# Where a step's work stands in the output stage of a long-convolution and mixture-of-experts kernel: number lists fetched later, measuring at the step's head, exponentials first

## The chip, the cores and the metric

The kernel runs on one core of a Trainium2 chip. The metric is device microseconds (us) of one launch, the median of several runs. Engines are named as the profile names them: PE (TensorE matmuls), PEld (its weight loads), DVE (VectorE), ACT (ScalarE), POOL (GpSimd) and SP (SyncE, which here only issues DMAs). Each engine works through its own instructions in order; between engines there are semaphores.

## The reference, cut to what matters

```python
def _attn_ref(x, v, pos_emb, w1, w2):            # x, v: 4 x 11456 x 128
    h_filt = (np.maximum(pos_emb @ w1, 0.0) @ w2) * np.exp(-0.01 * pos)[:, None]
    u = x * v
    ...                                           # y = causal convolution of u with h_filt, by FFT
    return x * y

def _moe_ref(x, w_skip, w_gate, w1, w2):          # x: 45824 x 128, 8 experts of 128 x 1024 x 128
    do_compute = x @ w_skip > 0                   # the others pass unchanged
    logits = xc @ w_gate
    e_idx = np.argmax(logits, axis=1)             # one expert for each token
    ...                                           # gate_w: its softmax probability
    for e in range(E):
        y[mask] = gate_w[mask, None] * (np.maximum(xc[mask] @ w1[e], 0.0) @ w2[e])
    out[do_compute] = xc + y
```

Everything is float32. The convolution's result is the input of the expert layer; which token goes to which expert is known only once its row of the convolution is there.

## The kernel before, in words

The program has four stages, one after the other. `first_phase` and `freq_phase` do the forward transforms and the product with the filter's spectrum; the change doesn't touch them. `out_phase` does the last transform, writes the rows, sorts the tokens to experts and begins the experts' work. `late_slots` does the rest of the experts.

`out_phase` goes through 32 chunks of 1,536 rows. A chunk's work is a set of small functions, each put at a *step* (the chunk's first step plus a lag) and at a rank within the step; the table of `(lag, order, f)` at lines 1336 to 1340 sets both. Chunks begin at steps 0, 4, 7 and then every third step (`START`, `first`), so chunk 2 begins at step 7, chunk 6 at 19, chunk 7 at 22 and chunk 8 at 25. Within a step the functions are issued in order of rank, and this is the order of the instructions on every engine. At rank 0.5 of every step (`PACE`: and now and then once more at the step's end) the generator `work` is advanced by one `yield`: that is the experts' work of `early_slots`, one part of a unit at a time.

What a chunk goes through: `produced` (lag 0: L1111 on PE multiplies with the transform, L1112 on DVE multiplies with x into the tile `xm`; the next loads of `ox` and half of the next `zt` are issued on SP), `turned` (lag 1, L1124: 12 transposes), `score` (lag 3, L1133, then ACT's copy `lt`, L1135), `score2` (lag 4, L1140), `choose` (lag 5, DVE: best expert, L1151 makes `df`), `exp` (L1165, ACT), `gate` (L1170 to L1172, DVE: writes the gate value into `xm`), `count` and `total` (PE: how many tokens go to each expert), `full` (L1191, DVE), `measure` (L1198, PE) and `measured`, `ranks` and `route`, `spread` (L1242, DVE), `collect` (L1250, PE), `write` (L1256, L1257 on DVE, then L615: POOL writes the chunk's token numbers to the lists in DRAM, one list for each expert). `store` writes `xm` to the output (SP, L1116). PE's products, scores and transposes share three PSUM buffers (`wide`, L1062), and the small results (`mine`, `whole`, `sizes`, `rk`, `tabs`) share one bank (L1034 to L1038).

The experts work in *slots* of 256 tokens of one expert. Which expert a slot takes, and where its numbers lie in the lists, is a *table*, made after chunks 2, 4, 8, 13, 22, 28 and 31 (`KNOWN`, `ex.table`, L557 to L606) in five *links* that alternate between DVE and PE; `tabled` advances it, up to two links a step. `name` then issues on SP the DMA that fetches a slot's 256 numbers (`ids<-lists`, L625), at most two slots a step, and not before the step after the chunk's list was written. `ex.more` issues on POOL the indirect DMAs that gather the rows by these numbers (`xt<-out,ids`, L667), one slot a step. `prepare` waits until a unit's slots are named, and for the first unit two more steps; then PE transposes the gathered rows (L719) and the unit's matmuls follow (L730 to L732 up, L813 down). 18 units of the first 28 slots belong to `early_slots`; what `out_phase` doesn't reach is done at its end without a chunk beside it (L1345 to L1356), and the other 61 slots and four half ones come in `late_slots`.

Of the kernel before, what the change touches and what calls it, by code (L numbers as in the profile page):

```python
# [44 lines left out]
NKNOWN = sum(n * u for c, n, u in KNOWN)  # L45
# [5 lines left out]
QX = 4  # L51
PACE = 1.24
START = (0, 4, 7)
STORE = 7
C4 = 2
XM = 4
ZT = 3
ZB = 2
# [4 lines left out]
NHALF = 4  # L63
NLAST = NEARLY + NLATE - NKNOWN
NTAB = 188
HALF = NKNOWN + NTAB
IDLE = 512
FRONT = 7
# [420 lines left out]
class Experts:  # L489
# [255 lines left out]
    def early_slots(self, pool, work, psum, bank):  # L745

        nc = self.nc

        def up(w, hl, u):
            n = hl.shape[2]  # L750
            hp = bank512()
            nf = 2 * T // n
            for f in range(nf):
                self.up(w, hl, hp[:, f * n:(f + 1) * n], u * nf + f)
            h = work.tile([128, 2 * T], F32, name="h", bufs=8)
            nc.scalar.activation(h, hp, AF.Relu)
            return [h[:, f * n:(f + 1) * n] for f in range(nf)]

        def bank512():
            return psum.tile([128, 2 * T], F32, name="mh")  # L760

        got, w, hl, wd = {}, {}, {}, {}
        self.ahead = got, w, hl

        self.now, seen = 0, []

        def gather(s, most=XT):
            while most and len(seen) < s + GATHERS and len(seen) in self.names:
                n = len(seen)
                seen.append(n)  # L770
                got[n] = self.gather(n, self.ids[:, n], pool, self.names[n])
                most -= 1

        self.more = lambda: gather(self.now, 1)

        def prepare(u):

            s = self.now = u[0]
            while not all(n in self.names for n in u):
                yield  # L780
            gather(s, max(u[-1] + 1 - len(seen), 0))
            if s not in hl:
                for _ in range(4 if s else 2):
                    yield
                w[s] = self.split(got[s][0], pool, 0, nc.vector)
                hl[s] = self.turn([got[n] for n in u], pool, bank512())
                yield
                if s:
                    yield
        for u, then in zip(BEFORE, BEFORE[1:] + UNITS[:1]):  # L790
            yield from prepare(u)
            s, k = u[0], then[0]
            sts = [got.pop(n) for n in u]
            wd[s] = work.tile([128, F], F32, name="wd", bufs=1)
            nc.scalar.copy(wd[s], self.w2f[:, ds(self.where(nc.scalar, sts[0][0]), F)])
            h, parts = [], 4 * len(u)
            for part in range(parts):
                h += up(w[s], hl[s], part)
                if part % 2 and part < parts - 1:
                    yield  # L800
            del w[s], hl[s]
            ready = all(n in got for n in then)
            if ready:
                w[k] = self.split_high(got[k][0], pool, 0)
                hp = bank512()
                hl[k] = self.turn_high([got[n] for n in then], pool, hp)
            yield
            if ready:
                self.turn_low(hl[k], hp)
                self.split_low(w[k], got[k][0], 0, nc.vector)  # L810
            for j in range(2 * len(u)):
                for f in range(F // 128):
                    nc.tensor.matmul(bank[:, j * D:(j + 1) * D], h[f][:, j * 128:(j + 1) * 128],  # L813
                                     wd[s][:, f * D:(f + 1) * D], start=(f == 0), stop=(f == F // 128 - 1))
                if j < 2 * len(u) - 1:
                    yield
            del wd[s]
            for m, (tb, xt, ids, since) in enumerate(sts):
                o = self.row()
                for j in range(2):  # L820
                    self.gated(o[:, j, 0:D], bank[:, (2 * m + j) * D:(2 * m + j + 1) * D], xt, j)
                    self.store(o[:, j], ids, j, since)
            yield
        yield from prepare(UNITS[0])

    def late_slots(self, pool):
# [205 lines left out]
def out_phase(tc, i, out, zd, ex, consts):  # L1032
# [6 lines left out]
    with (  # L1039
        tc.tile_pool(name="slot", bufs=2, reuse_waits="tile") as eb,  # L1040
    ):
      with (
# [16 lines left out]
        tabs = bank[0][:, 136:136 + 2 * NTAB]  # L1059
        revb = rev[:, None, :].broadcast_to([128, NT, E])  # L1060

        chunks = {}  # L1062
# [18 lines left out]
        def load_z(ch, p, heads=NP):  # L1081

            if ch < NCH:
                if ch not in zts:
                    zts[ch] = oz.tile([128, 2 * NP, NS * DH], F32, name="zt", bufs=ZB)
                rows = slice(p * NP, p * NP + heads)
                nc.sync.dma_start(zts[ch][:, rows], zs[2 * K1 * ch:2 * K1 * ch + 128, rows])
# [79 lines left out]
        def gate(ch):  # L1167
            xm, oh, ee, df = chunks[ch]
            sm = ob.tile([128, NT], F32, name="sm")
            nc.vector.tensor_reduce(sm, ee, axis=AX.X, op=ALU.add)  # L1170
            nc.vector.scalar_tensor_tensor(sm, sm, 1e-9, sm, ALU.add, ALU.max)
            nc.vector.reciprocal(xm[:, :, D], sm)  # L1172
            chunks[ch] = oh

        def count(ch):

            oh = chunks[ch][1]
            nc.tensor.matmul(mine, oh.rearrange("p e t -> p (e t)"), ones[:, 0:1], start=True, stop=True)

        def counted(ch):  # L1180
# [42 lines left out]
        def route(ch):  # L1223

            oh = chunks.pop(ch)
            sel = ob.tile([128, E, NT], F32, name="sel", bufs=1)
            nc.vector.scalar_tensor_tensor(sel, rk.rearrange("p (e t) -> p e t", t=NT), (PL + 1) / 2 / PL, oh, ALU.subtract, ALU.mult)
            rs = ob.tile([128, NT], F32, name="rs")
            nc.vector.tensor_reduce(rs, sel.rearrange("p e t -> p t e"), axis=AX.X, op=ALU.add)
            tf = ob.tile([128, 2, NT], F16, name="tf")  # L1230
            nc.vector.scalar_tensor_tensor(tf[:, 0], rs, WHOLE, wholes, ALU.add, ALU.subtract)
            nc.vector.tensor_tensor(tf[:, 1], rs, tf[:, 0], ALU.subtract)
            chunks[ch] = tf
# [27 lines left out]
        cr, cts, written, checks, base, at = {}, {}, {}, {}, 0, [0]  # L1261
# [16 lines left out]
        tables = []  # L1278
# [6 lines left out]
        def name(most=2):  # L1285

            for s, ch in fresh:
                ex.names[s] = ch
            fresh.clear()
            for _ in range(most):  # L1290
                if not groups:
                    return
                s, ch, b = groups[0]
                if b not in ex.tabled or written.get(ch, at[0]) >= at[0]:
                    return
                groups.pop(0)
                ex.issue(s, ch)
                fresh.append((s, ch))

        started = []  # L1300

        def tabled(half):

            if tables and (not half or started):
                started.append(1)
                if next(tables[0], tables) is tables:
                    tables.pop(0)
                    started.clear()

        def routed(ch):  # L1310
            route(ch)
            last = ch == NCH - 1
            if not last and ch in checks:
                tables.append(ex.table("full", *checks[ch], ob, tabs))
            if last:
                tables.append(zip_longest(ex.table("most", *checks[ch], ob, tabs), ex.table("half", HALF, NHALF, 1, ob, tabs[:, 64:])))
                tables.append(ex.table("last", NKNOWN, NTAB, 1, ob, tabs))

        def produced(ch):
            for blk in range(NB):  # L1320
# [11 lines left out]
        steps = {}  # L1332
        for ch in range(NCH):
            for blk in range(NB):
                steps.setdefault(first(ch) + blk + STORE, []).append((9, store, (ch, blk)))
            for lag, order, f in (
                    (0, 0, produced), (1, 0.1, lambda ch: load_z(ch + ZB, 1)), (1, 4, turned),
                    (3, -0.1, score), (4, 2, score2), (5, 3, choose), (6, 1, exp), (6, 4.5, count), (6, 6, counted), (6, 6, gate), (7, 4.4, total),
                    (8, -2.5, full), (8, 4.4, measure), (8, 4.5, ranks),
                    (9, -2.3, measured), (9, -2, routed), (11, -2.4, spread), (12, 0.2, collect), (12, 0.3, lay), (12, 2.5, laid), (12, 2.6, write)):  # L1340
                steps.setdefault(first(ch) + lag, []).append((order, f, (ch,)))
        for t in steps:
            steps[t] += [(-1.5, tabled, (0,)), (4.7, tabled, (1,)), (7.5, name, ()), (7.6, lambda: ex.more(), ())]
        credit = 0.0
        for t in sorted(steps):  # L1345
            at[0] = t
# [105 lines left out]
```

## Time and profile before

| | |
|---|---|
| median of 3 runs | 1577.55 us (1574.77 to 1578.71) |
| the profiled execution | 1581.42 us, of which its span is 1579.6 us |
| PE busy | 1484.2 us, 94% of the span |
| DVE, POOL, ACT busy | 72%, 68%, 48% |
| mean granted clock of TensorE | 0.973 of full speed |

The span is from the first instruction to the last; 1.8 us lie around it. Shares are means over stages with different limits, so the section with rows shows stretches of the span by themselves. A wait is told as "waiting engine and line <- what ended the wait". The granted clock is 1.00 at 2.4 GHz and 0.50 at 1.2 GHz.

### The profile page before, as it was taken

What the parts mean: (1) busy time and instruction counts of PE and PEld (TensorE: products, weight loads), DVE (VectorE), ACT (ScalarE), POOL (GpSimd) and SP (SyncE); (2) the same over time, 40 slices, a digit from 0 to 9 for tenths busy, and PEclk for the clock granted to TensorE, in tenths of its full rate; (3) what the DMA queues carried; (4) which work ended last, traced back from release to release, by engine and by line L of the source; (5) the groups of instructions that cost most, each with busy time, mean ns of one, the idle gap of its engine ahead of it and who ended that gap; (6) DMA issues with size and microseconds to landing.
All of it is one profiled execution on the core that took longest, in us unless ns stands there. A gap on an engine that the chain in (4) does not pass through costs nothing. (4 is left out here: it accounts for less than half of the span.)

```text
span 1579.6 us, 24184 instructions
## 1 busy us (share of the span) xinstructions
PE 1484.2 (94%) x7360; PEld 931.2 (59%) x7360; DVE 1130.7 (72%) x2323; ACT 755.1 (48%) x1509; POOL 1080.7 (68%) x832
## 2 busy tenths in 40 slices
PE   8976999999999999998759999999989999999998
PEld 3542444444444444443437767777777888888888
DVE  2324877888788889996757877777766777777774
ACT  5542555544545444442224554444535555555554
POOL 2102988888888878882157566875777888888756
PEclk9996999999999999999789999999989999999999
DMA  9998999999999978978968888988521111111100
GB/s 322 332 337 316 382 372 375 359 331 331 314 353 330 311 237 271 351 202 286 352 193 259 252 276 263 283 282 249 174 63 35 46 46 45 46 46 43 43 25 29
DMA packets 200376, 361.82 MB, mean 229 GB/s; under 512 B 64492, under 2 KB 140762, under 8 KB 200206
## 3 DMA queue, kind: packets, MB, share of 16 engines
q1 hardware_dynamic: 181078, 317.04, 59.5%
q0 software_dynamic: 16448, 38.88, 8.5%
q10 hardware_dynamic: 2720, 4.34, 0.9%
q8 instruction: 59, 0.97, 0.3%
q14 instruction: 71, 0.58, 0.1%
HBM read 216.77 MB, written 145.42 MB: 229 GB/s over the span
## 5 line engine op out<-in xcount | busy, mean ns | idle before, releaser
L412 PE MATMUL ps<-y,c 128*128 128x512 f32 x720 | 331.3, 597 | 0.3
L480 POOL TENSOR_TENSOR y<-y,p 128x2048 f32<-128x2048 f32 x59 | 267.8, 4538 | 70.0 <-DVE p L401 70.0
L736 POOL DMA_INDIRECT out<-o,ids x182 | 199.3, 1095 | 116.3 <-DVE o L743 78.6
L412 PEld LDWEIGHTS ps<-y,c 128*128 128x128 f32 x720 | 133.4, 190 | 173.0 <-issue 156.5
L667 POOL DMA_INDIRECT xt<-out,ids x182 | 192.8, 1059 | 58.4 <-issue 29.1
L401 DVE TENSOR_TENSOR p<-xp,g 128x1024 f32<-128x1024 f32 x240 | 217.4, 948 | 0.0
L401 DVE TENSOR_TENSOR y<-xp,g 128x1536 f32<-128x1536 f32 x120 | 210.9, 1757 | 4.0
L852 DVE SCALAR_TENSOR_TENSOR hh<-hp,hh 128x1024 fp32r<-128x1024 f32 x122 | 148.7, 1219 | 88.9 <-ACT hh L851 75.5
L413 ACT COPY z<-ps 128x512 f32<-128x512 f32 x180 | 105.6, 586 | 178.3 <-PE ps L412 158.6
L851 ACT ACTIVATE hh<-hp 128x1024 fp32r<-128x1024 f32 x122 | 126.4, 1036 | 92.1 <-issue 70.4
L481 POOL TENSOR_TENSOR y<-y,p 128x1024 f32<-128x1024 f32 x59 | 139.1, 2357 | 4.6
L640 POOL MEMSET idle<- 128x512 f16 x231 | 126.3, 547 | 0.3
L381 PE MATMUL xp<-x,wf 128*128 128x480 f32 x256 | 117.4, 583 | 9.1 <-DMA x<-x1f 5.9
L210 PE MATMUL ps<-wf,c 60*120 60x384 f32 x512 | 112.6, 536 | 11.6 <-DVE wf L193 11.6
L212 ACT COPY wf<-ps 120x384 f32<-120x384 f32 x256 | 105.6, 493 | 27.0 <-PE ps L210 23.8
L813 PE MATMUL bank<-wd,h 128*128 128x128 f32 x896 | 114.8, 286 | 0.0
L193 POOL TENSOR_TENSOR wf<-wf 124x768 f32<-124x768 f32 x45 | 82.0, 1822 | 47.5 <-DVE g L394 47.4
L813 PEld LDWEIGHTS bank<-wd,h 128*128 128x128 f32 x896 | 108.0, 198 | 0.3
L730 PE MATMUL hp<-hl,ws 128*128 128x512 f32 (+1 forms) x256 | 103.2, 403 | 2.6 <-issue 1.5
L393 DVE TENSOR_TENSOR g<-xp,g 128x128 f32<-128x128 f32 x120 | 34.8, 290 | 97.2 <-ACT g L386 97.1
L384 ACT COPY g<-xp 64x192 f32<-64x192 f32 x120 | 38.0, 317 | 137.4 <-PE xp L381 94.7
L707 DVE TENSOR_TENSOR ws<-wf,ws 128x1024 fp32r<-128x1024 f32 x82 | 99.9, 1218 | 5.0 <-issue 3.2
(199 smaller groups left out, 2851.3 us busy)
## 6 DMA issues: line engine op xcount, KB each, us to landing
wf<-xv SPq DMA_DIRECT2D x64, 768.0 KB
x1d<-wf SPq DMA_DIRECT2D x64, 720.0 KB
x<-x1d SPq DMA_DIRECT2D x60, 768.0 KB
zt<-zd SPq DMA_DIRECT2D x60, 768.0 KB
zd<-z SPq DMA_DIRECT2D x110, 384.0 KB
out<-xm SPq DMA_DIRECT2D x96, 258.0 KB
ox<-xo SPq DMA_DIRECT2D x96, 256.0 KB
x1f<-fx POOLq DMA_DIRECT2D x16, 720.0 KB
```

The source lines that it names most:

```text
L210: nc.tensor.matmul(ps[p], self.c1[rows], u[rows, q * RUN:(q + 1) * RUN], start=True, stop=True)
L381: nc.tensor.matmul(xp[:, k, 0:(NS + NB) * DH], c2(n % PER * KS + j * KH + k), x1[:, j * KH + k], start=True, stop=True)
L401: nc.vector.tensor_tensor(o[:, :, :, j * KH:(j + 1) * KH].rearrange("p s a k b d -> p (s a) k b d"), x[:, None].broadcast_to([128, m, KH, ...
L412: nc.tensor.matmul(zps, c3[:, a, :], y[:, blk, a], start=(a == 0), stop=(a == 1))
L480: nc.gpsimd.tensor_tensor(y[:, 1:], y[:, 1:], p1, ALU.add)
L481: nc.gpsimd.tensor_tensor(y[:, 2:], y[:, 2:], p2, ALU.add)
L640: self.nc.gpsimd.memset(self.idle, 0.0)
L667: ins = nc.gpsimd.indirect_dma_start(out=xt[:, j], out_offset=None, in_=self.rows[0:have], in_offset=bass.IndirectOffsetOnAxis(ap=ids[:, j ...
L736: ins = nc.gpsimd.indirect_dma_start(out=self.rows, out_offset=bass.IndirectOffsetOnAxis(ap=ids[:, j:j + 1], axis=0), in_=o, in_offset=Non ...
L813: nc.tensor.matmul(bank[:, j * D:(j + 1) * D], h[f][:, j * 128:(j + 1) * 128], wd[s][:, f * D:(f + 1) * D], start=(f == 0), stop=(f == F / ...
L851: nc.scalar.activation(h[:, 0], hp, AF.Relu)
L852: nc.vector.scalar_tensor_tensor(h[:, 1], hp, 0.0, h[:, 0].bitcast(F32), ALU.max, ALU.subtract)
```

## The change

Eight edits, all in `out_phase` and `early_slots`:

- `STORE` 7 becomes 6: a block of `xm` is stored one step earlier.
- The first unit waits three steps instead of two after its numbers are named (L783).
- `name` fetches numbers two steps behind the list's writing instead of one.
- `exp` moves to the head of its step, ahead of the score's copy; `gate` from the step's end to its middle. `count` now takes the chunk's state over from `exp`.
- `measure` and `ranks` move from the end of the step at lag 8 to the head of lag 9, just ahead of `measured`.
- Tables of chunks 7 to 30 (`FRONT` is 7) advance one link a step, the others two as before; the first of the two places in a step moves from rank -1.5 to -0.1.
- `score2` moves behind the step's transposes (`turned`).
- The second half of a `zt` load moves from the next step's head to its own step's end, ahead of the stores there.

```diff
-STORE = 7
+STORE = 6
...
-                for _ in range(4 if s else 2):
+                for _ in range(4 if s else 3):
...
-            chunks[ch] = oh
...
-            oh = chunks[ch][1]
+            oh = chunks[ch] = chunks[ch][1]
...
-                if b not in ex.tabled or written.get(ch, at[0]) >= at[0]:
+                if b not in ex.tabled or written.get(ch, at[0]) >= at[0] - 1:
...
-            if tables and (not half or started):
+            if tables and (not half or started and tables[0][1]):
                 started.append(1)
-                if next(tables[0], tables) is tables:
+                if next(tables[0][0], tables) is tables:
...
-                tables.append(ex.table("full", *checks[ch], ob, tabs))
+                tables.append((ex.table("full", *checks[ch], ob, tabs), ch < FRONT))
...
-                    (0, 0, produced), (1, 0.1, lambda ch: load_z(ch + ZB, 1)), (1, 4, turned),
-                    (3, -0.1, score), (4, 2, score2), (5, 3, choose), (6, 1, exp), (6, 4.5, count), (6, 6, counted), (6, 6, gate), (7, 4.4, total),
-                    (8, -2.5, full), (8, 4.4, measure), (8, 4.5, ranks),
-                    (9, -2.3, measured), (9, -2, routed), (11, -2.4, spread), (12, 0.2, collect), (12, 0.3, lay), (12, 2.5, laid), (12, 2.6, write)):
+                    (0, 0, produced), (0, 8.9, lambda ch: load_z(ch + ZB, 1)), (1, 4, turned),
+                    (3, -0.05, score), (4, 4.2, score2), (5, 3, choose), (6, -0.5, exp), (6, 2.7, gate), (6, 4.5, count), (6, 6, counted), (7, 4.4, total),
+                    (8, -2.5, full), (9, -0.4, measure), (9, -0.35, ranks),
+                    (9, -0.3, measured), (9, -0.2, routed), (11, -2.4, spread), (12, 0.2, collect), (12, 0.3, lay), (12, 2.5, laid), (12, 2.6, write)):
...
-            steps[t] += [(-1.5, tabled, (0,)), (4.7, tabled, (1,)), (7.5, name, ()), (7.6, lambda: ex.more(), ())]
+            steps[t] += [(-0.1, tabled, (0,)), (4.7, tabled, (1,)), (7.5, name, ()), (7.6, lambda: ex.more(), ())]
```

What moves on the engines, at three places. First PE, where the first slot's gathered rows (`xt`) are transposed. Before, this is at the head of chunk 7's second step, behind a count of tokens (L1178) and one link of a table (L571, L572); `score2` and the chunk's transposes come after:

```order
L1213 MATMUL bank_4480<-ge_4482 53x1
L1178 LDWEIGHTS oh
L1178 MATMUL bank_4478<-ones,oh 96x1
L571 LDWEIGHTS shift
L571 MATMUL bank_4478<-tnt,shift 8x1
L572 LDWEIGHTS shift
L572 MATMUL bank_4478<-done,shift 8x1
L719 MATMUL mh<-ident,xt_4442 128x128 x2
L1140 MATMUL bank_4480<-ident,lt 128x128 x3
L1124 MATMUL wide<-ident,xm 128x128 x12
```

Of the change, the same transposes (L719), now at the head of chunk 8's second step, and with `score2` (L1140) behind the chunk's transposes:

```order
L1212 MATMUL bank_4480<-ge_4481 53x1
L1177 LDWEIGHTS oh
L1177 MATMUL bank_4478<-ones,oh 96x1
L719 MATMUL mh<-ident,xt_4442 128x128 x2
L1124 MATMUL wide<-ident,xm 128x128 x12
L1140 MATMUL bank_4480<-ident,lt 128x128 x3
L1185 LDWEIGHTS odd
L1185 MATMUL bank_4478<-ct,odd 96x1
L730 MATMUL mh<-hl,ws_5522 128x256
```

The first unit has moved by one chunk on PE: chunk 8's score, product and collecting now stand ahead of it.

Second SP, ahead of the first fetch of numbers (L623 loads the slot's address, L625 fetches). Before, it follows the loads that chunk 6's steps issue, with one store between the two halves of `zt`:

```order
L1078 DMA ox<-xo 128x512 x3
L1087 DMA zt<-zd 128x4x384
L1116 DMA out<-xm 128x516
L1087 DMA zt<-zd 128x4x384
L623 TENSOR_LOAD addr
L623 ISA x2
L625 REGISTER_ALU
L625 DMA ids<-lists 128x2
```

Of the change, the same place: both halves of `zt` go out together, and two stores stand between them and the first fetch:

```order
L1078 DMA ox<-xo 128x512 x3
L1087 DMA zt<-zd 128x4x384 x2
L1116 DMA out<-xm 128x516 x2
L623 TENSOR_LOAD addr
L623 ISA x2
L625 REGISTER_ALU
L625 DMA ids<-lists 128x2
```

The fetch has moved behind the stores, to just ahead of the loads that chunk 7's steps issue.

Third ACT, a chunk with a unit beside it. Before, the score's copy (`lt`) stands ahead of the unit's work (`h`, `ws`, `hl`), and `exp` (`ee`) behind it:

```order
L1135 COPY lt<-wide 128x384
L756 ACTIVATE h<-mh 128x512 x2
L691 TENSOR_LOAD tb
L691 ISA x2
L702 ISA
L702 COPY ws_5577<-wf 128x1024
L721 CAST hl<-mh 128x256
L1165 ACTIVATE ee<-df 128x96
L1182 CAST ct<-bank_4478 96x1
L1142 COPY lg<-bank_4480 128x108
L1127 COPY xT<-wide 128x512 x3
```

Of the change:

```order
L702 COPY ws_5631<-wf 128x1024
L721 CAST hl<-mh 128x256
L1165 ACTIVATE ee<-df 128x96
L1135 COPY lt<-wide 128x384
L1181 CAST ct<-bank_4478 96x1
L1127 COPY xT<-wide 128x512 x3
L1142 COPY lg<-bank_4480 128x108
```

`exp` now stands directly ahead of the score's copy, and `lg` behind the three copies `xT`.

## Rows read from the trace of the kernel before

**Rows 1.** Stretches of the span: its bounds and length in us, busy us of each engine (and instructions), granted clock, busy share of the DMA engines, GB/s.

```profile
730.00:800.00 70.00, 52.93 (x352) 27.05 (x353) 46.06 (x170) 18.15 (x45) 9.82 (x10) 0.88 0.94 318
800.00:820.00 20.00, 5.37 (x34) 4.86 (x34) 6.70 (x27) 4.14 (x8) 12.59 (x14) 0.66 0.70 220
820.00:1130.00 310.00, 298.43 (x2452) 221.01 (x2451) 233.48 (x882) 145.42 (x297) 211.02 (x245) 1.00 0.82 258
1130.00:1200.00 70.00, 61.91 (x431) 50.99 (x431) 44.72 (x183) 29.61 (x49) 55.14 (x65) 0.93 0.27 64
1200.00:1500.00 300.00, 299.07 (x1412) 246.79 (x1411) 222.28 (x323) 174.03 (x204) 239.09 (x248) 1.00 0.16 44
```

**Rows 2.** Waits of PE from 700 to 1200 us: total us, times, longest us.

```profile
PE mh L719 <- DMA xt<-out,ids: 13.8, 2, 9.7
...
PE bank L1140 <- DVE pl L1257: 5.1, 4, 3.0
PE bank L1198 <- DVE tdn L599: 4.5, 3, 1.8
PE bank L1198 <- DVE tab L594: 3.9, 3, 2.1
```

**Rows 3.** Timeline of PE around the first slot's transposes: start, us, instruction, and in brackets the idle time before it and what ended it.

```profile
793.31 1.47 PE L1124 MATMUL wide<-ident,xm 128*128 128x128 f32 x12
...
800.81 0.16 PE L572 MATMUL bank<-done,shift 8*8 8x1 f16 x1
810.63 0.48 PE L719 MATMUL mh<-ident,xt 128*128 128x128 f32 x1 [9.65 <-DMA xt<-out,ids]
815.29 0.47 PE L719 MATMUL mh<-ident,xt 128*128 128x128 f32 x1 [4.19 <-DMA xt<-out,ids]
815.56 0.85 PE L1140 MATMUL bank<-ident,lt 128*128 128x128 f32 x3
816.20 2.52 PE L1124 MATMUL wide<-ident,xm 128*128 128x128 f32 x12
```

**Rows 4.** Two short stretches within that wait, columns as in rows 1.

```profile
805.00:810.00 5.00, 0.00 (x0) 0.00 (x0) 1.23 (x1) 0.00 (x0) 4.34 (x5) 0.50 0.59 147
810.00:815.00 5.00, 0.48 (x1) 0.18 (x1) 0.00 (x0) 0.00 (x0) 4.67 (x6) 0.50 1.00 329
```

**Rows 5.** Timeline of POOL there: the writing of chunk 2's list and the first two gathers.

```profile
793.18 1.59 POOL L615 DMA_INDIRECT lists<-pl,lies  x1 [7.37 <-DVE sm L1170]
...
805.28 2.12 POOL L667 DMA_INDIRECT xt<-out,ids  x1 [7.72 <-DMA ids<-lists]
...
808.12 1.02 POOL L667 DMA_INDIRECT xt<-out,ids  x1 [0.17 <-issue]
```

**Rows 6.** Timeline of SP's DMA issues there: the last load before the first fetch, and the fetch.

```profile
793.93 0.42 SPq L1087 DMA_DIRECT2D zt<-zd  x1
802.56 1.46 SPq L625 DMA_DIRECT2D ids<-lists  x2
```

**Rows 7.** Timeline of DVE: the products (L1112) of chunks 5, 6 and 7, and the wait of `full` between the first two.

```profile
777.12 1.89 DVE L1112 TENSOR_TENSOR xm<-wide,ox 128x512 f32<-128x512 f32 x3 [0.96 <-DMA out<-xm]
...
783.10 0.15 DVE L1191 TENSOR_SCALAR nt<-bank 96x1 int32<-96x1 f32 x1 [1.23 <-PE bank L587]
...
789.62 0.69 DVE L1112 TENSOR_TENSOR xm<-wide,ox 128x512 f32<-128x512 f32 x1
...
800.79 1.89 DVE L1112 TENSOR_TENSOR xm<-wide,ox 128x512 f32<-128x512 f32 x3
```

**Rows 8.** Timeline of PE in the same stretch: `score2`, `measure` and the products of chunks 6 and 7.

```profile
779.43 0.90 PE L1140 MATMUL bank<-ident,lt 128*128 128x128 f32 x3 [3.04 <-DVE pl L1257]
...
785.19 0.22 PE L1198 MATMUL bank<-ct,sums 96*128 96x2 f16 x3 [2.13 <-DVE tab L594]
...
786.96 4.79 PE L1111 MATMUL wide<-zt,c 128*64 128x512 f32 x12
...
792.92 0.55 PE L1140 MATMUL bank<-ident,lt 128*128 128x128 f32 x3 [0.63 <-DVE pl L1257]
...
796.47 2.80 PE L1111 MATMUL wide<-zt,c 128*64 128x512 f32 x12
```

**Rows 9.** Timeline of PE: the first and the last of `measure`'s waits for a table from 820 us on (of five).

```profile
821.02 0.21 PE L1198 MATMUL bank<-ct,sums 96*128 96x2 f16 x3 [0.50 <-DVE tab L594]
...
1136.72 0.21 PE L1198 MATMUL bank<-ct,sums 96*128 96x2 f16 x3 [1.78 <-DVE tdn L599]
```

**Rows 10.** Timeline of PE: score and product of one chunk with experts' work beside it.

```profile
928.76 0.85 PE L1133 MATMUL wide<-xT,wg 128*32 128x384 f32 x8
929.55 2.79 PE L1111 MATMUL wide<-zt,c 128*64 128x512 f32 x12
```

**Rows 11.** Timeline of ACT beside it: the score's copy and `exp`.

```profile
929.68 0.48 ACT L1135 COPY lt<-wide 128x384 f32<-128x384 f32 x1 [1.11 <-PE wide L1133]
931.66 0.28 ACT L1165 ACTIVATE ee<-df 128x96 f32<-128x96 f32 x1 [1.50 <-DVE df L1151]
```

**Rows 12.** Timeline of PE at the stage's end: down matmuls (L813) of the last unit but one, and the first up and the down matmuls of the last unit.

```profile
1167.44 8.41 PE L813 MATMUL bank<-wd,h 128*128 128x128 f32 x48
...
1178.44 0.50 PE L730 MATMUL mh<-hl,ws 128*128 128x512 f32 x1
...
1185.79 7.31 PE L813 MATMUL bank<-wd,h 128*128 128x128 f32 x64
```

More of the change, by code (lines that the diff above doesn't have):

```diff
@@ L1313, in routed @@
             if not last and ch in checks:
-                tables.append(ex.table("full", *checks[ch], ob, tabs))
+                tables.append((ex.table("full", *checks[ch], ob, tabs), ch < FRONT))
             if last:
-                tables.append(zip_longest(ex.table("most", *checks[ch], ob, tabs), ex.table("half", HALF, NHALF, 1, ob, tabs[:, 64:])))
-                tables.append(ex.table("last", NKNOWN, NTAB, 1, ob, tabs))
+                tables.append((zip_longest(ex.table("most", *checks[ch], ob, tabs), ex.table("half", HALF, NHALF, 1, ob, tabs[:, 64:])), True))
+                tables.append((ex.table("last", NKNOWN, NTAB, 1, ob, tabs), True))
         def produced(ch):
```

## The prediction

> **What bounds the kernel now.** I read the stretches first, then PE's waits, then the timelines around the longest of them. The reader is to see in the stretches [rows 1] three regimes of the stage that changes. From 730 to 800 us PE is busy 52.9 of 70 us, the DMA engines 0.94 and DVE 46.1: loads and DVE set the pace, not PE. From 820 to 1130 PE is busy 298.4 of 310 us and after 1200 it is 299.1 of 300: there PE is the bound, and whatever time PE loses earlier comes out at the end. Between them PE does 5.4 us of work in 20. So I price the change by the time in which PE stands still or runs slowly from 730 us on, and ask of each such wait whether it goes.
>
> The longest is the first slot's gathered rows: 13.8 us in two waits [rows 2, 3]. Behind it the granted clock is 0.50, the lower level [rows 4], and the first transposes take 2.52 us where they took 1.47 before: 1.05 us more [rows 3]. Then come `score2` waiting for DVE's `pl` (5.1 us) and `measure` waiting for the tables (4.5 and 3.9 us) [rows 2].
>
> **The change part by part.** The durations come from the profiled execution of 1581.42 us, 3.87 us above the median of the runs; I subtract from it and take the 3.87 off at the end.
>
> *Fetching later, one more step for the first unit.* Counted through the loops, chunk 2's list is written in step 19; before, the numbers are fetched at the end of step 20, gathered at the end of step 21 and used on PE in step 23; now this is 21, 22 and 26. The chain itself is long: POOL issues the list at 793.18 [rows 5]; SP, idle since 794.35, issues the fetch at 802.56 [rows 6], 9.4 us later; the first gather starts at 805.28, the second at 808.12 [rows 5], and its rows are there at 815.29 [rows 3]. That is 22.1 us from list to transposes. How much of it do the later places cover? The list is issued 3.56 us after chunk 6's first product on DVE (789.62), and PE comes to its place in step 26 at about chunk 8's product, two chunks on. Chunk 6 to 7 took 11.17 us on DVE [rows 7] and 9.51 us on PE [rows 8]. Two chunks less 3.56 are 18.8 us at the one pace and 15.5 at the other, so 3.3 to 6.6 us of the wait stay; I take 5.0, and for the range 0 to the whole 13.84. So 8.8 us go. The slow restart stays in the sum, as a wait of 3.04 us at 779 also left products at 4.79 us instead of 2.80 [rows 8]. The Trainium skill ("TensorE: Matmul & The Clock Gate", section "HAM oscillation — how this bites in real kernels") says that idle gaps throttle the array again and that each restart is paid; the trace agrees with the 4.79 us, and if the leftover wait spared it the sum would be 1.05 us lower. Against the gain stands that the units begin two steps later, in the regime where PE idles: 17.1 of 70 us [rows 1], 0.24, of two thirds of a 9.5 us chunk are 1.5 us. **First unit: 8.8 - 1.5 = 7.3 us.**
>
> What the later fetch does to SP: it now stands ahead of chunk 8's `ox`, but it is reached later, so the 8.2 us between 794.35 and 802.56, in which nothing behind it is loaded, become a wait of perhaps half as much. The Trainium skill ("DMA: Bandwidth & Descriptors", "Latency and other measured facts") puts a DMA's fixed cost at about 2 us and lower on a lightly loaded HBM. By it the list would have landed near 796.8, an estimate; the trace shows the fetch 7.8 us after POOL had issued the list, so I keep the row. By the page the leftover wait would be 0 and the sum 5.0 us lower.
>
> *Store a step earlier, `score2` behind the transposes, in the DVE-paced stretch.* Here a stall of PE is worth only what it costs DVE. DVE waited 0.96 us for an output store to free `xm` and 1.23 us for PE's total, which stood behind the waiting `score2` and the slowed transposes [rows 7, 8]. With `STORE` 6 the store has a step more, and `pl` is ready by the time the transposes are done. The rest of the 3.04 and 2.13 us is DVE's own pace and stays. **2.2 us.** Bounds: 0, and the 5.2 us of both PE waits.
>
> *One link a step, measuring at the head, `score2` later, in the PE-bound stretch.* `score2`'s waits there are 5.1 less 3.04 and 0.63 [rows 2, 8], 1.4 us; `measure`'s are 4.5 plus 3.9 less 2.13 [rows 2, 8], 6.3 us in five waits [rows 9]. A table's last link no longer stands right ahead of `measure`: it falls in a chunk's second step, and a unit's part and 12 transposes come before PE next writes that bank. All 7.7 us go. What is late next: `exp` is now ahead of the score's copy on ACT. PE's third product needs the PSUM buffer that this copy frees (three buffers, score and two products before it). In the chunk at 929 `exp` could only start at 931.66, for DVE's `df` [rows 11]; with 0.28 and 0.48 behind it the buffer is free at 932.4, and PE would want it at 929.55 + two thirds of 2.79 = 931.4 [rows 10]: a new wait of 1.0 us. DVE lags so far in few chunks; I take two such waits, 2.0 us. **5.7 us.** Bounds: 0 and 7.7.
>
> *`gate` in the middle, `count`, `measured`, the second `zt` half.* Nothing: DVE's order around `measured` is the same and PE's `measure` still precedes score and product; the `zt` half is needed two chunks later. What hides them is the experts' matmuls, and from 730 to 800 us, where there are none, they are within the 2.2 us above.
>
> *The stage's end.* The last units start three steps later and more of their matmuls fall behind the last chunk. PE does them at the same cost wherever they stand, unless it idles. From 1130 to 1200 PE idles 8.1 us at a mean clock of 0.93 [rows 1]. I take 0, bounds a gain of 5 us (70 us times 0.07 of clock) and a loss of 14 us (a rival, below).
>
> **Sum:** 7.3 + 2.2 + 5.7 = 15.2 us. 1581.4 - 15.2 = 1566.2, less 3.9 for the median: **1562 us**, 1.0% faster.
>
> **The rivals.**
>
> *The wait moves along whole.* The list may land later under a busier DMA queue: the DMA engines are at 0.94 in this stretch [rows 1] and were at 0.59 for part of the chain [rows 4]. For it: everything up to the gather is fed by a DMA. Against it: the program gives 15 to 19 us where the chain took 22. Then 8.8 us don't come: 1571 us.
>
> *The gain is used up at the end.* The last unit's matmuls took from 1178.44 to 1193.1, some 14 us, at full clock; the 48 down matmuls ahead of them took 8.41 us where 64 take 7.31 [rows 12], 0.175 us each instead of 0.114. Should PE idle so long before the last unit that it runs at half the clock throughout, its 14 us double: 1576 us. For it: three parts fewer lie beside a chunk. Against it: more experts' work, not less, then stands beside the last tables.
>
> *Slower: `exp` holds up every product.* If in each of the 24 chunks from chunk 8 on DVE is as late as at 929, PE waits 1.0 us in each for its third product: 24 us instead of the 2 counted, 1562 + 22 = 1584 us. It decides from a `df` that ends more than 1.9 us after the score's start: then 0.28 and 0.48 put the copy's end past the 2.65 us [rows 10, 11] at which the third product is due. For it: DVE is 75% busy there [rows 1]. Against it: `exp` was behind a unit's copies before, and `gate` behind that; with `exp` early DVE waits less and lags less.
>
> **How the numbers follow.** The forecast 0.66, with a range of its own from 1554 to 1570; the wait moved along 0.14, the end 0.08, slower 0.07; better than the range's lower end 0.05. A measurement of this kernel can tell 0.3%, 4.7 us, from no change. The forecast, the better case and half of the moved wait, whose 1571 lies near the bound of 1572.8, are faster: 0.78. The other half and the end are the same: 0.15. Slower: 0.07. The range goes down by the whole leftover wait and the clock at the end, 1562 - 5 - 5 = 1552, and up by the whole wait and the third term, 1562 + 8.8 + 5.7 = 1577.
>
> **What would show it.** Right: PE's wait at L719 is some 5 us instead of 13.8; `measure` and `score2` are gone from PE's list of waits; PE from 820 to 1130 is busy over 0.97; the first long matmuls of the late stage start 12 to 18 us earlier. Wrong: a wait of 10 us or more at L719; PE waiting at L1111 for ACT's `lt`; a granted clock near 0.5 for over 15 us between 1130 and 1200; SP held so long by the fetch that products wait for `ox`.

## The result, and the profile after

The changed kernel is slower: 1591.3 us, median of 7 runs (1590.81 to 1595.93), against 1577.55 us for the kernel before on the same chip (7 runs, 1572.4 to 1584.92). The ratio is 1.0096, 95% interval [1.0073, 1.0119]: 0.96% slower, where 1.0% faster was forecast and the range ended at 1577. The profiled execution took 1594.65 us, its span 1592.8 us, the mean granted clock fell from 0.973 to 0.965.

The same five stretches as in [rows 1], of the kernel after:

```profile
730.00:800.00 70.00, 55.71 (x369) 27.47 (x370) 49.22 (x185) 19.03 (x50) 10.31 (x11) 0.88 0.97 330
800.00:820.00 20.00, 13.76 (x99) 9.14 (x101) 15.93 (x57) 7.68 (x16) 18.40 (x22) 0.83 0.99 311
820.00:1130.00 310.00, 289.92 (x2305) 210.08 (x2299) 219.24 (x832) 137.41 (x284) 207.90 (x238) 0.97 0.81 249
1130.00:1200.00 70.00, 61.00 (x449) 50.77 (x450) 41.64 (x178) 25.51 (x45) 46.93 (x56) 0.90 0.25 58
1200.00:1500.00 300.00, 297.98 (x1417) 245.93 (x1416) 220.83 (x323) 171.98 (x200) 238.27 (x250) 1.00 0.17 44
```

Up to 820 us PE has more to do, as the prediction said: it is busy 69.5 of 90 us instead of 58.3. Most of that difference belongs to the one profile of [rows 1], though: a second profile of the kernel before (experiment 8) has 66.4. In the long stretch from 820 to 1130, where PE is the bound and was to gain 5.7 us, it is busy 289.92 us instead of 298.43 and the clock is 0.97 instead of 1.00. The late stage begins 10.5 us later (L863, its first down matmul, at 1212.91; 1202.44 before, and 1197.2 in the second profile). PE's waits from 700 to 1220 us, which answer to [rows 2], say where:

```profile
PE bank L585 <- DVE sel L1226: 12.7, 4, 4.3
...
PE bank L1197 <- DVE trow L590: 2.7, 1, 2.7
...
PE bank L1197 <- DVE tstep L575: 2.2, 2, 1.1
...
PE bank L1197 <- DVE tab L594: 2.1, 1, 2.1
```

Gone are the gathered rows (13.8 us), `score2` waiting for `pl` and `measure` waiting for `tdn`; `measure` (here L1197) still waits 7.0 us for tables, where it waited 8.4. New, and the longest of all, is L585: the fourth link of a table, four times. It waits for DVE's `sel`, which has nothing to do with tables. PE's timeline at the second of the four (chunk 13's table; the score and product answer to [rows 10]):

```profile
935.19 0.22 PE L1197 MATMUL bank<-ct,sums 96*128 96x2 f16 x3
935.27 0.20 PE L1219 MATMUL bank<-oh,tri 128*128 128x96 f16 x1
935.32 0.21 PE L1220 MATMUL bank<-cols,ct 96*128 96x96 f16 x1
939.82 0.16 PE L585 MATMUL bank<-tph,onesf 8*1 8x7 f16 x1 [4.30 <-DVE sel L1226]
...
939.99 1.51 PE L1133 MATMUL wide<-xT,wg 128*32 128x384 f32 x8
941.43 4.24 PE L1111 MATMUL wide<-zt,c 128*64 128x512 f32 x12
```

DVE at the same place:

```profile
934.61 0.16 DVE L582 CAST tph<-tpast 8x7 f16<-8x7 f32 x1
...
934.69 0.67 DVE L725 TENSOR_TENSOR hl<-mh,hl 128x512 fp32r<-128x512 f32 x1
935.73 1.23 DVE L707 TENSOR_TENSOR ws<-wf,ws 128x1024 fp32r<-128x1024 f32 x1 [0.37 <-issue]
...
938.41 0.60 DVE L743 SCALAR_TENSOR_TENSOR o<-bank,xt 128x128 f32<-128x128 f32 x2
...
939.53 0.24 DVE L1226 SCALAR_TENSOR_TENSOR sel<-bank,oh 128x96 f32<-128x96 f32 x1
```

What the fourth link needs, `tph` of the third, ends at 934.77, before PE even begins `measure`. But PE issues the link right behind `ranks` (L1219, L1220), which has just written `rk` into the bank that the tables share, and the link is held until DVE has read `rk` (`sel`). DVE comes to that only behind a unit's split (L725, L707), `choose`, two outputs (L743) and `measured`. The runs show that the wait goes with the bank (experiment 5); whether the chip asks for it or only the program's own order of reads and writes in a bank, none of them tells. So PE stands 4.30 us, and then the score takes 1.51 us and the product 4.24 where 0.85 and 2.79 stood in [rows 10]: 2.1 us more, which is the clock. Windows around the four waits (columns as in rows 1):

```profile
860.00:870.00 10.00, 6.06 (x49) 4.06 (x48) 6.47 (x28) 4.51 (x9) 4.06 (x4) 0.79 0.73 237
870.00:880.00 10.00, 10.00 (x77) 7.27 (x74) 4.46 (x20) 4.01 (x9) 2.11 (x2) 0.87 0.61 180
930.00:940.00 10.00, 5.70 (x60) 5.57 (x58) 7.37 (x28) 3.46 (x8) 3.27 (x4) 0.88 0.89 284
940.00:950.00 10.00, 10.00 (x58) 5.07 (x56) 4.84 (x22) 4.00 (x8) 4.19 (x6) 0.78 0.42 125
...
1060.00:1070.00 10.00, 9.70 (x60) 5.12 (x60) 5.32 (x26) 3.00 (x7) 6.93 (x9) 0.83 0.46 139
1140.00:1150.00 10.00, 7.55 (x42) 5.29 (x42) 5.18 (x32) 3.02 (x6) 8.14 (x10) 0.66 0.22 79
```

At full clock these windows would read 1.00. What is missing, times 10 us, is 2.1 + 1.3 + 1.2 + 2.2 + 1.7 + 3.4 = 11.9 us of clock. Part of it costs nothing beyond the wait, since at the first two places the clock falls while PE still stands:

```profile
866.00:867.00 1.00, 0.00 (x0) 0.00 (x0) 0.89 (x6) 0.00 (x0) 0.00 (x0) 0.50 0.92 316
938.00:939.00 1.00, 0.00 (x0) 0.00 (x0) 0.94 (x5) 0.00 (x0) 0.00 (x0) 0.50 0.82 286
```

From the fall of the clock to the end of the wait it is 1.7 and 2.3 us, at half the clock 2.0 us of the 11.9. That leaves 9.9 us of clock beside the 12.7 us of waits: some 23 us in all.

Why the fourth link? A chunk begins every third step. A table's first link is issued at rank -0.1 of the step in which its chunk's `measured` stands; with one link a step the fourth falls three steps later, at the same rank of the next chunk's step, and there `measure` (-0.4), `ranks` (-0.35), `measured` (-0.3) and `routed` (-0.2) have just been issued. With two links a step all five are over before that step comes.

### The profile page after: what moved, and what is told of

Read it like the earlier page. It is cut to its first block, busy times and chain, and to the rows that moved or that the text cites. A ratio compares the mean times of both kernels' runs of the same rounds, so it can differ in the third digit from the quotient of the medians.

```text
span 1592.8 us, 24190 instructions
## 1 busy us (share of the span) xinstructions
PE 1496.2 (94%) x7360; PEld 932.0 (59%) x7360; DVE 1131.0 (71%) x2323; ACT 751.7 (47%) x1509; POOL 1081.4 (68%) x832
## 5 line engine op out<-in xcount | busy, mean ns | idle before, releaser
L210 PE MATMUL ps<-wf,c 60*120 60x384 f32 x512 | 113.6, 539 | 11.2 <-DVE wf L193 11.2
L813 PE MATMUL bank<-wd,h 128*128 128x128 f32 x896 | 112.0, 282 | 0.0
L615 POOL DMA_INDIRECT lists<-pl,lies x32 | 51.0, 1593 | 89.0 <-DVE sm L1170 61.0
L1111 PE MATMUL wide<-zt,c 128*64 128x512 f32 x384 | 102.1, 654 | 7.8 <-DMA zt<-zd 5.7
L813 PEld LDWEIGHTS bank<-wd,h 128*128 128x128 f32 x896 | 105.2, 194 | 0.6 <-issue 0.2
```

Of the source, the lines that this page charges most:

```text
L210: nc.tensor.matmul(ps[p], self.c1[rows], u[rows, q * RUN:(q + 1) * RUN], start=True, stop=True)
```

## The experiments

The theory (A): the place of the fourth link costs some 20 us, by a wait on a bank and not on data. The rivals: (B) measuring at a step's head puts PE behind DVE, whatever the tables do; (C) the deferral costs it, since units, fetch and tables all come later, and the experts' work is put off to the end. A second question within A is whether the pace of one link a step or its place decides. Experiments 1 to 4 ran on a chip on which the kernel before took 1593.3 us, 5 to 8 and 9 to 12 on two others with 1577.51 and 1575.94 us, so ratios to the kernel before on the same chip are compared, not times; the times in the texts on what was expected are those of the change's chip.

| experiment | edit | ratio to before, 95% interval |
|---|---|---|
| the change | | 1.0096 [1.0073, 1.0119] |
| 1 | change, two links a step | 0.9960 [0.9938, 0.9982] |
| 2 | change, the one link at the step's middle | 1.0029 [1.0005, 1.0053] |
| 3 | change, `measure` and `ranks` as before | 1.0089 [1.0058, 1.0119] |
| 4 | before, later fetch alone | 0.9983 [0.9958, 1.0008] |
| 5 | change, tables in another bank | 0.9993 [0.9977, 1.0010] |
| 6 | as 1, early fetch | 0.9951 [0.9934, 0.9967] |
| 7 | before, one link a step alone | 1.0099 [1.0069, 1.0129] |
| 8 | before once more | one run |
| 9 | as 1, again | 0.9967 [0.9955, 0.9979] |
| 10 | as 6, again | 0.9953 [0.9936, 0.9969] |
| 11 | as 6, `exp` and `gate` as before | 0.9949 [0.9933, 0.9964] |
| 12 | as 6, `score2` as before | 0.9971 [0.9958, 0.9983] |

**1. Two links a step for every table, the rest of the change kept.**

```diff
-tables.append((ex.table("full", *checks[ch], ob, tabs), ch < FRONT))
+tables.append((ex.table("full", *checks[ch], ob, tabs), True))
```

> The changed kernel with every table advanced at both places of a step, as before. Theory A (place of the link): PE's four waits at L585 for DVE's reading of the ranks, 12.7 us, and the half clock behind them, about 12 us, come from the fourth link standing at a step's head; without the one-link rule the fourth link stands behind the product, those waits go and the time falls to 1565 to 1573 us. Theory B (measuring at the head): the waits come from the later measuring; the time stays above 1585 us. Theory C (experts' work put off to the end): 1585 us or more, since nothing of that changes.

0.9960 instead of 1.0096: one rule of eight edits costs 1.4%, some 21 us, and without it the change is faster than the kernel before. The waits of L585 for `sel` are gone, and the clock there is whole, as three of the windows show:

```profile
870.00:880.00 10.00, 10.00 (x93) 7.38 (x91) 6.64 (x23) 5.23 (x12) 4.77 (x6) 1.00 0.85 255
...
940.00:950.00 10.00, 10.00 (x83) 7.81 (x79) 7.14 (x27) 4.16 (x9) 4.53 (x4) 1.00 0.85 256
...
1060.00:1070.00 10.00, 9.16 (x85) 8.49 (x86) 7.17 (x29) 2.76 (x8) 2.14 (x2) 1.00 0.62 186
```

`measure` still stands at the step's head here, so B falls.

**2. One link a step, but at rank 4.7 instead of -0.1.**

```diff
-            if tables and (not half or started and tables[0][1]):
+            if tables and ((not half or started) if tables[0][1] else half):
```

> The changed kernel with one link a step for the later tables, but at the middle of the step (rank 4.7) instead of its head. Theory A, the place: like the two links, 1565 to 1575 us, no wait at L585 over 1 us. Theory A', the pace (tables finished later starve the experts): no better than the changed kernel, 1588 us or more. Theory B: above 1585 us.

1.0029, neither of the forecasts: about half of what experiment 1 gives back comes back. PE's list of waits shows what remains:

```profile
PE bank L1197 <- DVE tstep L575: 7.6, 4, 2.6
```

The bank is now held the other way round: `measure` stands behind the second link of the table and waits until DVE has read it (L575). With five links drawn over five steps, some link meets a chunk's measuring in the shared bank; that the place only decides how long the wait is, is read from the order and not tested further.

**3. `measure` and `ranks` back at the end of the step at lag 8.**

```diff
-                    (8, -2.5, full), (9, -0.4, measure), (9, -0.35, ranks),
+                    (8, -2.5, full), (8, 4.4, measure), (8, 4.5, ranks),
```

> The changed kernel with measure and ranks back at the end of the step before (ranks 4.4 and 4.5). Theory A: the fourth link still stands behind DVE's reading of the ranks at the head, and the waits at L585 shrink little, 1585 to 1593 us. Theory B: the loss is gone, 1565 to 1573 us.

1.0089, the intervals nearly coincide with the change's. The wait of L585 for `sel` stays at 11.2 us in four. B falls here too: `ranks` half a step earlier doesn't help, since DVE reads `rk` at the head of lag 9 in both.

**4. The kernel before with the later fetch and the third step for the first unit, nothing else.**

```diff
-                for _ in range(4 if s else 2):
+                for _ in range(4 if s else 3):
...
-                if b not in ex.tabled or written.get(ch, at[0]) >= at[0]:
+                if b not in ex.tabled or written.get(ch, at[0]) >= at[0] - 1:
```

> The kernel before with two edits alone: numbers fetched two steps behind the list, and three steps' wait for the first unit. If the first gather's wait (13.8 us) is what the fetch gains and the units' later begin costs little, 1563 to 1571 us; if the later begin of the units costs what the wait was worth (theory C), 1576 us or more. A is silent on it.

0.9983, with 1 inside the interval: no cost, so the later units and fetch can't be the 15 us of C (its later tables are answered by experiment 5, which keeps them late); but hardly a gain either, though the wait for the gathered rows is gone from the list. Experiments 9 and 10 come back to this.

**5. All tables but chunk 31's in another bank, the order of the instructions unchanged.**

```diff
-        e, r = ps[0:1, 0:limit], ps[0:1, NTAB:NTAB + limit]
+        wide = 24 if kind == "full" else NTAB
+        e, r = ps[0:1, 0:limit], ps[0:1, wide:wide + limit]
...
-tables.append((ex.table("full", *checks[ch], ob, tabs), ch < FRONT))
+tables.append((ex.table("full", *checks[ch], ob, bank[2][:, 420:468]), ch < FRONT))
```

> The changed kernel with the same order of instructions, but the tables of chunks 2 to 28 use columns of the third small PSUM bank instead of the first, which holds the ranks that DVE reads at the head of a step. Theory A1 (the fourth link waits only because it writes the bank that DVE is still reading): the waits at L585 of 2.6 to 4.3 us go, the half clock behind them too, and the time is 18 to 28 us below the changed kernel, at or below the two links, 0.990 to 0.998 of the kernel before. Theory A2 (the link waits for its own table's numbers, or for its place in DVE's order): the waits stay and the time is within 5 us of the changed kernel, 1.006 or more.

0.9993: 16 us come back with every instruction in its place, a little less than the 18 to 28 expected. Line numbers are one higher here than in the change. PE's waits of this run:

```profile
PE bank L572 <- DVE pl L1257: 8.6, 4, 3.0
...
PE bank L586 <- DVE tph L583: 3.7, 3, 1.8
```

The fourth link of these tables (here L586) now waits only for its own input `tph`, 3.7 us. That is the direct evidence that the wait for `sel` is one on the bank. `measure`'s waits for tables are gone as well. The new bank has a reader of its own: the second link (L572) waits for `pl`, 8.6 us, which is likely why this doesn't reach experiment 1.

**6. As 1, and the fetch and the first unit's two steps as before.**

```diff
-                for _ in range(4 if s else 3):
+                for _ in range(4 if s else 2):
...
-                if b not in ex.tabled or written.get(ch, at[0]) >= at[0] - 1:
+                if b not in ex.tabled or written.get(ch, at[0]) >= at[0]:
```

> The two-link kernel with the numbers fetched one step behind the list again and two steps' wait for the first unit. If the fetch's term is 7.3 us and the others work beside it: the first gather's wait is back at 10 to 14 us and the time is 4 to 9 us above the two-link kernel, 1.000 or a little below of the kernel before. If the later fetch gained nothing in the end, the time equals the two-link kernel's, 0.996.

0.9951, 1569.6 us, which beats both kernels, although PE waits 9.5 us for the gathered rows again. So it came out as if the later fetch gained nothing in the end.

**7. The kernel before with the one-link rule alone.** `tables` holds pairs as in the change; all ranks are as before.

```diff
-            if tables and (not half or started):
+            if tables and (not half or started and tables[0][1]):
...
-                tables.append(ex.table("full", *checks[ch], ob, tabs))
+                tables.append((ex.table("full", *checks[ch], ob, tabs), ch < FRONT))
```

> The kernel before with the one-link rule alone. Theory A: its links at a step's head (rank -1.5, behind DVE's reading of the ranks) bring PE waits at L585 of 2 to 4 us in four tables, and it is 8 to 22 us slower than before. Rival: only together with measuring at the head does the link wait; then within 4 us of before.

1.0099: alone on the kernel before, the rule costs 15 us, as much as the whole change loses; the rival falls, since `measure` stands at its old place here. Its line, of this run:

```profile
PE bank L585 <- DVE sel L1227: 9.3, 4, 3.0
```

**8. The kernel before, unchanged, profiled once more.**

> The kernel before, unchanged, for a profile of the same chip: the late experts' stage and the end behind the last store, to tell what of it differs with the chip. The first late down matmul is expected within 1 us of 1202.4, as in the first profile.

It took 1575.22 us, its span 1573.4. Its late stage begins at 1197.2, 5 us earlier than in the first profile, not within 1 us. The wait that headed [rows 2] was little more than half as long:

```profile
PE mh L719 <- DMA xt<-out,ids: 7.7, 2, 5.3
```

**9 and 10. Experiments 1 and 6 again, side by side on one chip.**

> Every table two links a step, fetch two steps behind the list, as tried before, now beside its twin with the early fetch on one chip. If the later fetch is worth the gather's wait that it removes (9.5 us with the early fetch here), this one is 6 to 9 us faster than its twin. If the wait is only exchanged for work that begins later, the two are within 4 us of each other.

> The twin: fetch one step behind the list, two steps' wait for the first unit. Some 0.995 of the kernel before, as measured once. If the later fetch pays, this one is slower than its twin by 6 to 9 us, else the same within 4.

1571.64 us with the later fetch, 1569.59 with the early one: within 4 us, and if anything the wrong way. So the wait is exchanged, not gained. Two views show for what. First, the start of the late stage, the first L863 on PE, of 9 and then of 10:

```profile
1190.35 0.39 PE L863 MATMUL my<-hh,ws 128*128 128x512 f32 x1
```

```profile
1195.35 0.40 PE L863 MATMUL my<-hh,ws 128*128 128x512 f32 x1
```

Run 6, the same kernel as 10, had it at 1189.89, and 11 and 12, also with the early fetch, at 1190.35 and 1196.09. With 12.3 us of waits for gathered rows in 10, 9.5 in 6 and none in 9, the later fetch brings the late stage forward by some 2 us on the mean of 6 and 10, which is less than the 6 us by which these profiles differ among themselves. Second, the end. The last instruction on POOL, of 9 and of 10:

```profile
core 0 of [0], span 1569.9 us
...
1561.75 0.54 POOL L640 MEMSET idle<- 128x512 f16 x1
```

```profile
core 0 of [0], span 1571.6 us
...
1566.78 0.54 POOL L640 MEMSET idle<- 128x512 f16 x1
```

From its end to the end of the span it is 7.6 us in 9 and 4.3 in 10. All seven profiles with the later fetch and the third step of the first unit (the change, 1 to 5, 9) show 7.6, the seven without these two edits (the kernel before twice, 6, 7, 10 to 12) 4.3. SP's waits show where most of these 3.3 us lie: at the program's end (L1447, the line that starts the program), where the engines wait for one another. Of 9 and of 10:

```profile
SPq L1447 <- PEq L1447: 5.2, 2, 4.7
```

```profile
SPq L1447 <- PEq L1447: 2.5, 2, 2.0
```

In the trace's records it is POOL that comes last there: its instruction `DRAIN` takes 3.91 us in all seven with the later fetch and 1.21 in the others, and an `INC_SWDGE_SEM` ahead of it 1.13 to 1.14 against 0.47 to 0.49. Why it takes longer no run shows.

The stretches of 9 from 820 us on, beside those of the change, also give the sum of the loss:

```profile
820.00:1130.00 310.00, 299.61 (x2442) 222.47 (x2438) 232.99 (x887) 143.99 (x300) 213.58 (x247) 0.99 0.81 254
1130.00:1200.00 70.00, 62.36 (x405) 51.17 (x406) 42.68 (x135) 29.85 (x42) 57.51 (x68) 0.95 0.25 51
```

The change has 9.7 and 1.4 us less PE work in them. It also lacks more clock, 8.5 and 3.4 us summed over the steps of the clock in the two traces (the two decimals shown here give the first only to some 3 us). Less the 2.0 us that lie in waits this is some 21 us, against 22.6 us by which its late stage begins later (1212.91 and 1190.35). From the first L863 to POOL's last start it is 371.7 us in the one and 371.4 in the other, so nothing was lost behind.

**11. As 6, `exp` behind the score's copy and `gate` at the step's end, as before.** The hand-over of the chunk's state between `gate` and `count`, not shown, goes back with them.

```diff
-                    (3, -0.05, score), (4, 4.2, score2), (5, 3, choose), (6, -0.5, exp), (6, 2.7, gate), (6, 4.5, count), (6, 6, counted), (7, 4.4, total),
+                    (3, -0.1, score), (4, 4.2, score2), (5, 3, choose), (6, 1, exp), (6, 4.5, count), (6, 6, counted), (6, 6, gate), (7, 4.4, total),
```

> The early-fetch twin with exp behind the score's copy again (lag 6, rank 1), gate at the step's end and the score at rank -0.1. The prediction held that exp ahead of the copy costs two waits of 1.0 us and gains nothing: then this is 2 us faster than the twin and the waits of the product for lt are gone. A rival holds that the early gate gives something back (gate value written sooner, store and list earlier): then this is slower than the twin by 2 us or more.

1568.0 against 1569.59 us, the intervals overlap: inconclusive between 2 us and nothing, but not the rival. The mechanism is there. PE's timeline of 9, with `exp` early, shows the third product of a chunk waiting for the copy `lt`, as the prediction described it:

```profile
928.70 0.85 PE L1133 MATMUL wide<-xT,wg 128*32 128x384 f32 x8
929.48 1.94 PE L1111 MATMUL wide<-zt,c 128*64 128x512 f32 x8
932.00 1.08 PE L1111 MATMUL wide<-zt,c 128*64 128x512 f32 x4 [0.58 <-ACT lt L1135]
```

Over the stage this is 1.6 us in two waits in the change and 3.4 in four in 10; in 11 it doesn't appear among PE's longest.

**12. As 6, `score2` ahead of the step's transposes, as before.**

```diff
-                    (3, -0.05, score), (4, 4.2, score2), (5, 3, choose),
+                    (3, -0.05, score), (4, 2, score2), (5, 3, choose),
```

> The early-fetch twin with score2 ahead of the step's transposes again (lag 4, rank 2). By the prediction's terms (5.1 us of waits of score2 for pl, of which 3.5 us count as DVE's own pace) this is slower than the twin by 1.4 us at least, and by up to 5 us if the waits counted in full; score2's wait for pl comes back as some 5 us in four waits. If the place of score2 is worth nothing, the two agree within 2 us.

1572.12 against 1569.59 us: 2.5 us slower, and its wait for `pl` is back, 3.2 us in three. The intervals overlap, so the sign is likely and the size rough.

## Why the prediction was wrong

**The step that failed** is in the third term: "A table's last link no longer stands right ahead of `measure`... All 7.7 us go." I followed the fifth link and asked what PE does before it next writes the bank. The fourth link writes the same bank on PE, and it was not followed: it falls right behind `ranks`, at a place where DVE is 2.6 to 4.3 us from reading what `ranks` wrote. The old waits did shrink (from 820 us on `measure`'s were priced at 6.3 us; now its waits for a later table are the 2.2 us for `tstep`), but 12.7 us of waits with 9.9 us of clock came: a term put at a gain of 5.7 us held a cost of some 22.6. Experiments 1, 5 and 7 show it from three sides: without the rule the loss is gone, with the same order and another bank most of it, and the rule alone makes it. The working asked for the bank's next writer behind the fifth link, and not for its readers ahead of the fourth. Its own rows had waits of this kind: in [rows 7] DVE's `full` waits for L587, a matmul of a table's fourth link whose result it doesn't read, and the working took this for the total (L1186), which ended 0.2 us earlier.

**First unit, 7.3 us.** That the later fetch removes the wait was right, and more fully than said: L719 starts without waiting, where 5.0 us were to be left. Of the change:

```profile
810.30 0.42 PE L719 MATMUL mh<-ident,xt 128*128 128x128 f32 x2
```

Two chunks took PE 21.8 us in the changed kernel (products at 784.59 and 806.41), not 19.0, so that L719 comes 20.1 us behind the list's writing (790.16), where 15.5 to 18.8 were counted. The list itself landed little sooner: SP's fetch begins 6.3 us after POOL's writing ended (791.75 to 798.08), 7.8 before. But the gain was mis-sized on both sides. The 13.84 us was one draw: seven profiles with the early fetch show 13.8, 7.7, 9.5, 9.6, 12.3, 11.8 and 7.5, mean 10.3. And "the units begin two steps later... 1.5 us" was far too small, beyond the slip that its own count (step 23 becomes 26) makes three steps, 2.3 us: of the 10.3 us some 2 at most can be seen at the start of the late stage, so some 8 are used up on the way, and 3.3 go at the program's end. Experiments 9 and 10 put the term at -2 us, 4 at +2.7; neither can be told from 0. How the 8 us divide between the later units and the work that filled the wait was not taken apart.

**DVE-paced start, 2.2 us, and `score2` and `exp` in the third term.** With the rule undone and the early fetch back (10), what is left of the change gains 0.47%, 7.4 us. Of that `score2`'s place is some 2.5 us, a rough size (12); the prediction had 1.4 in the third term and a part of the 2.2. `exp` was priced at a cost of 2.0 us in two waits; measured, 1.2 to 3.4 us of waits and no change that can be told from none (11). The other 5 us or so lie with the earlier store, the `zt` half, the tables' first place and `measure`; they weren't separated, except that `measure` back at its old place changed nothing in the company of the one-link rule (3). That the 7.4 us lie near the 7.9 of the two terms is partly luck: 6.3 of them were to come from the one link a step, and `measure`'s waits for tables from 820 us on fall to 2.0 to 3.3 us with two links as well (1, 6, 9, 10).

**The end, 0.** Right for the late stage, which is as long as ever from its first matmul to its last store. The clock from 1130 to 1200 is 0.90 (the kernel before has 0.93 and, in its second profile, 0.90): half of what is missing lies behind the table at 1142, the other half from 1170 to 1176, behind PE's waits of 2.61 and 1.12 us for the tables of chunk 31. The 3.3 us at the program's end were not foreseen.

**The rivals.** The wait didn't move along. The last units' clock was not halved. `exp` holds up a few products, not every one: the direction of the third rival came true by another mechanism, which was not on the list, and its 0.07 was the whole chance given to slower. The signs named as right were met at L719 and for `score2`. They failed for `measure`, whose waits for tables stay in the list with 7.0 us, for the start of the late stage, which is 10.5 us later and not 12 to 18 earlier, and at "busy over 0.97" (289.92 of 310 is 0.935), which was the sign that counted. Of the signs named as wrong one appeared, PE waiting at L1111 for `lt`, with 1.6 us.

## What to carry to other kernels

When a change spreads a chain of small steps over more time, follow every link of it to its new neighbours on each engine, not the first and last only; where the chain's period is that of the surrounding loop, as three one-link steps are here, one link always lands on the same neighbour. For each write of PE into a shared PSUM bank ask which engine still has to read something else there, and how far that engine is behind; a wait for an instruction that doesn't make the operand, as L585's for `sel`, is the sign of it in a profile. And before a single wait carries half of a forecast, compare it over several executions, and ask what fills the time once it is gone.

## What the runs showed of the hardware

PE's four waits of 2.6 to 4.3 us cost nearly as much again in clock: 12.7 us of waits came with 9.9 us of clock beside them, at granted clocks of 0.66 to 0.88 in the windows above, while the windows at the first three places read 1.00 in experiment 1. The Trainium skill ("TensorE: Matmul & The Clock Gate", "HAM oscillation — how this bites in real kernels") says that idle gaps throttle the array and each restart is paid; the trace agrees, and here the restarts were 9.9 of some 22.6 us. The first gather's wait varies from 7.5 to 13.8 us between executions in which PE's order up to it is nearly the same. And the end of the span behind POOL's last memset has two lengths, 4.3 and 7.6 us, which go with the later fetch and the first unit's third step; most of the difference is POOL's `DRAIN`, 1.21 or 3.91 us, and its cause stays open.
